# Two DRAM bounces of batch 2 issued ahead of the output weights, in a fused attention and snake-MLP kernel

## The chip, the cores and the metric

The kernel runs on one core of one Trainium2 chip. The metric is the device time in microseconds of one execution, the median over several runs. The profile is of one further execution, with its own time. In the code batches count from 0, so "the third batch" of the change is batch 2; the numbers below are those of the code.

## The reference

Attention with a relative-position bias over 8 batches, 8 heads, 576 positions and head size 64, and then a two-layer network with the snake activation on its 4608 x 512 result:

```python
scores = scale * np.matmul(q, k.transpose(0, 1, 3, 2))
scores = scores + bias.transpose(2, 0, 1)[None, :, :, :]
scores = scores - np.max(scores, axis=-1, keepdims=True)
attn = np.exp(scores)
attn = attn / (np.sum(attn, axis=-1, keepdims=True) + 1e-09)
x = np.matmul(attn, v)            # heads side by side: 4608 x 512
h = x @ w_in                      # 512 x 2048
s = np.sin(alpha * h)
g = h + s * s / (alpha + 1e-09)
return (g @ w_out).astype(np.float32)   # 2048 x 512
```

All inputs are float32; the kernel computes in float16 with float32 sums.

## The kernel before

**Stages.** The kernel goes through the batches t = 0 to 7. Attention of a batch runs over four pairs of heads p. For each pair TensorE (PE) forms the transposed scores (`sc`, from `kT` and `qT`, key chunks 0 to 3, a tail `t` from `kt`, and chunk 4 with the last 64 queries), ScalarE takes the exponential into `u` (L705), VectorE multiplies the part near the diagonal by the bias factor `m2r` or `mhr` (L730, L713), PE multiplies by `v` and `vh` into `am` (the attention-value products), and VectorE divides by the sums (L784, L785). The result goes transposed into `xT`: for batch 0 with PE and a copy, from batch 1 on with a transposing DMA on SP from `xp` (L815).

The network works on blocks b of 512 tokens. Input matmuls give 16 chunks of h (`sc<-xT,w_in`), ScalarE takes the sine (L865), ScalarE or VectorE the square (L872, L874), and VectorE adds it to h in `g` (L879), which also frees the PSUM bank of that chunk. Output matmuls (`am<-w_out,g`) sum over the 16 chunks f of `g` for each of four groups of 128 tokens, a copy to `outs` follows (L536, L538) and a DMA to `out` (L929). Block 0 is put in after the attention of batch 0; after batch 1 there is none, and block 1 follows the attention of batch 2. So the attention of batches 1 and 2 comes back to back, and the 64 output matmuls of block 0 are spread through it as filling work (L919, `fill`).

**Who sets the order.** The order of instructions on each engine is fixed when the kernel is built. `Plan` keeps tasks with estimated durations, dependences, priorities and a due time `nb` before which the plan does not start them, and emits them in the order in which its own clock would run them. On the chip only that order and the semaphores count; the due times act through the order alone. Some due times stand for the landing of a DMA that is issued outside the plan: `T_TR1` for the natural loads of k and q of batch 1, `T_V` for v of batches 0 and 1, `T_WO` for the four quarters of `w_out` (quarter f // 4 for output matmul f).

**The DMA queues.** Loads that change float32 to float16 go through POOL, whose DMA instructions share one software queue (q0). SP issues through a hardware queue (q1): transposing loads, copies of the tail of `kT` into `kt` (L385), and the results. The opening part of POOL is written out by hand, ahead of the plan. It ends with `load_w_in16`, two natural loads of k and q for batch 1 (`nat2`, L426), `load_v32(1)` (six loads to `v1st`, L408 and L411), `load_w_out16` (four quarters, L436) and `cast_v(1)` (six casts of `v1st` to `v` and `vh`, L416 and L419). `v1st` is needed because `w_out16` lends its space to v of batch 0 until that is cast.

From batch 2 on, k and q take another way. `stage_kq(t)` (L377) copies k and q of batch t from DRAM to DRAM, as float16 with the heads side by side (`staged_k`, `staged_q`): these are the bounces. `load_kqT(t)` then has SP load them transposed into `kT` (L389) and `qT` (L390) and fills `kt`. The buffers of `kT`, `qT`, `kt`, `v` and `vh` are double, by t % 2. For batch 2 the bounce is issued in `first` of batch 0, at the start of its scores in the plan, which on POOL's queue is behind `cast_v(1)`; `load_v16(2)`, `load_kqT(2)` and `stage_kq(3)` come in `first` of batch 1. From batch 3 on a task of the plan on SP, `ahead`, does this.

## Time and profile before

| | us |
|---|---|
| median of 8 runs | 394.9 |
| lowest and highest run | 391.36, 396.79 |
| the profiled execution, its own time | 392.74 |
| its span in the profile | 391.0 |

The span covers all but 1.7 us of the profiled execution's own time. All times inside the execution are microseconds from the start of the span. TensorE ran at full clock throughout.

| DMA (POOL) | issued at | time to landing |
|---|---|---|
| `nat2` k, q | 21.77, 22.55 | 14.5, 16.7 |
| last load to `v1st` | 33.72 | 10.7 |
| `w_out`, four quarters | 36.59, 39.58, 41.03, 41.97 | 10.1, 9.7, 11.1, 12.5 |
| `staged_k`, `staged_q`, batch 2 | 46.16, 47.89 | 12.1, 14.1 |
| `staged_k`, `staged_q`, batch 3 | 58.72, 62.41 | 19.0, 22.9 |

On SP, the transposing loads of batch 2 hold the queue from 58.30 (`kT`, 5.95) and from 64.31 (`qT`, 7.73).

How to read it: an issue is the time at which POOL writes the descriptors, the landing is when the semaphore tells that all data have arrived; with a queue that is full most of the time to landing is spent behind other DMAs. In a busy row "x" counts instructions. In a chain of work each line is start, length and what ran; a line that names a DMA is time in which the chain waited for that transfer. In a row of DMA packets the columns are packets, megabytes and the time that the packets took as a share of 16 engines; with several packets in flight on one engine that share goes over 100%.

### The profile page before, as it was taken

Reading aid. Unit: us, or ns where it says so; the run is one execution under the profiler, and the core shown is the slowest. Engines: PE = TensorE matmul, PEld = TensorE weight load, DVE = VectorE, ACT = ScalarE, POOL = GpSimd, SP = SyncE. Lnnn points to the kernel's source line nnn. Section 1 sums busy time; section 2 is a strip of 40 time slices with the busy share of each in tenths; the row PEclk is TensorE's granted clock in tenths of the full one; section 3 lists DMA queues with packets and bytes.
Section 4 is the critical chain, followed back from the end, with each engine's and each line's share of the span. In section 5 each row is a group of like instructions: output and inputs, shape, how many; then the busy total and the mean of one; then the engine's idle time right before and its main releaser. Section 6 shows DMA issues by size and latency. Waiting matters only on the chain.

```text
span 391.0 us, 8534 instructions
## 1 busy us (share of the span) xinstructions
PE 375.2 (96%) x3381; PEld 188.2 (48%) x3381; DVE 261.6 (67%) x584; ACT 322.5 (82%) x453; POOL 82.3 (21%) x96
## 2 busy tenths in 40 slices
PE   5989899999999999999999999999999999999995
PEld 2456445455544554455445544554455444444442
DVE  3676986767886679668966786679667949429100
ACT  2876999899999999999999999999999959539211
POOL 5672864063720044006300310000000000000000
PEclk9999999999999999999999999999999999999999
DMA  9999999999999969949992397210121000020112
GB/s 164 198 207 219 209 176 149 151 185 151 147 162 158 150 90 149 186 75 90 133 172 77 38 66 183 85 24 9 54 57 50 14 27 28 29 80 2 60 74 80
DMA packets 151207, 42.58 MB, mean 109 GB/s; under 512 B 140344, under 2 KB 145552, under 8 KB 151168
## 3 DMA queue, kind: packets, MB, share of 16 engines
q0 software_dynamic: 89872, 19.04, 58.9%
q1 hardware_dynamic: 61072, 22.95, 32.0%
q8 instruction: 26, 0.43, 0.5%
q14 instruction: 13, 0.11, 0.1%
q10 hardware_dynamic: 224, 0.05, 0.1%
HBM read 37.76 MB, written 16.52 MB: 139 GB/s over the span
## 4 chain that ended last, share of the span: by engine, by line
PE 82%; DMA 8%; ACT 4%; DVE 3%; issue 1%; POOL 1%; ACTq 0%; SPq 0%; DVEq 0%
PE sc L450 40%; PE am L450 34%; PE ca L450 4%; PE cb L450 4%; ACT u L705 3%; DMA qT<-staged_q 3%; DMA m2r<-e_dram 2%; DMA e_dram<-e_sb 1%; DMA phi_sb<-phi_const 1%; DVE g L879 1%; DVE outs L538 0%; DVE kT L538 0%; DVE xp L785 0%; POOL mhr L471 0%; DVE sq L874 0%
## 5 line engine op out<-in xcount | busy, mean ns | idle before, releaser
L705 ACT ACTIVATE u<-sc 128x1024 f16<-128x1024 f32 (+1 forms) x192 | 157.3, 897 | 14.1 <-PE sc L450 12.5
L450 PE MATMUL sc<-xT,w_in 128*128 128x512 f16 x576 | 132.6, 379 | 0.9 <-DVE g L879 0.6
L879 DVE SCALAR_TENSOR_TENSOR g<-sq,inv_a,sc 128x512 f16<-128x512 f16 x144 | 103.1, 745 | 24.0 <-PE am L450 16.6
L450 PE MATMUL am<-w_out,g 128*128 128x512 f16 x448 | 116.2, 380 | 0.3 <-DVE outs L538 0.2
L865 ACT ACTIVATE s<-sc,alphaT 128x512 f16<-128x512 f32 x144 | 93.0, 678 | 5.5 <-PE sc L450 4.2
L730 DVE TENSOR_TENSOR u<-u,m2r 128x512 f16<-128x512 f16 (+2 forms) x160 | 68.1, 440 | 31.5 <-ACT u L705 27.0
L450 PEld LDWEIGHTS <-w_in 128*128 128x128 f16 x576 | 55.2, 98 | 64.9 <-issue 1.8
L450 PEld LDWEIGHTS <-g 128*128 128x128 f16 x576 | 53.4, 98 | 66.2 <-issue 12.5
L450 PEld LDWEIGHTS <-u 128*128 128x128 f16 x1440 | 55.8, 98 | 17.2 <-issue 8.7
L450 PE MATMUL am<-v,u 128*128 128x65 f16 x1216 | 53.6, 194 | 0.0
L450 PE MATMUL sc<-qT,kT 64*128 64x64 f16 (+1 forms) x512 | 49.3, 295 | 2.8 <-ACT u L705 1.9
L872 ACT ACTIVATE sq<-s 128x512 f16<-128x512 f16 x79 | 49.2, 628 | 2.2 <-DVE g L879 0.5
L396 POOL DMA_DIRECT2D v<-in_v_dram x24 | 22.2, 1064 | 117.2 <-PE am L450 117.2
L450 PE MATMUL am<-vh,u 128*128 128x130 f16 x152 | 33.9, 223 | 1.0 <-DVE xp L785 0.8
L874 DVE TENSOR_TENSOR sq<-s 128x512 f16<-128x512 f16 x65 | 27.7, 428 | 5.2 <-ACT s L865 4.4
L450 PEld LDWEIGHTS <-kT 64*128 64x128 f16 x512 | 14.6, 95 | 29.9 <-issue 25.6
L785 DVE TENSOR_TENSOR xp<-am,rd 128x384 f16<-128x384 f32 (+1 forms) x56 | 27.5, 491 | 2.0
L784 DVE RECIPROCAL rd<-am 128x6 f32<-128x6 f32 (+1 forms) x60 | 11.2, 186 | 22.6 <-PE am L450 22.2
L538 DVE COPY outs<-am 128x512 f32<-128x512 f32 x21 | 14.4, 688 | 6.1 <-PE am L450 6.0
L937 ACT ACT_TABLE_LOAD x13 | 16.7, 1283 | 0.2
L377 POOL DMA_DIRECT2D staged_q<-in_q_dram x6 | 15.5, 2583 | 4.4 <-DMA staged_q<-in_q_dram 4.4
L536 ACT ACTIVATE outs<-am 128x512 f32<-128x512 f32 x7 | 4.2, 594 | 13.6 <-PE am L450 13.6
(87 smaller groups left out, 167.9 us busy)
## 6 DMA issues: line engine op xcount, KB each, us to landing
out_dram<-outs SPq DMA_DIRECT2D x36, 256.0 KB, 2.2
staged_k<-in_k_dram POOLq DMA_DIRECT2D x6, 576.0 KB, 16.5
staged_q<-in_q_dram POOLq DMA_DIRECT2D x6, 576.0 KB, 20.8
v<-in_v_dram POOLq DMA_DIRECT2D x24, 128.0 KB, 6.8
w_in<-in_moe_w_in_dram POOLq DMA_DIRECT2D x4, 512.0 KB, 9.7
w_out<-in_moe_w_out_dram POOLq DMA_DIRECT2D x4, 512.0 KB, 10.6
xT<-xp SPq DMA_TRANSPOSE x72, 3.5
w_out<-in_v_dram SPq DMA_DIRECT2D x4, 256.0 KB, 8.6
```

The costliest lines, as they stand in the source:

```text
L377: nc.gpsimd.dma_start(out=dst.ap()[t].rearrange("s (h d) -> s h d", h=H), in_=src[t].rearrange("h s d -> s h d"),)
L396: nc.gpsimd.dma_start(out=vs[t % 2][:, c, :, 0:D], in_=vp[128 * c : 128 * c + 128],)
L450: nc.tensor.matmul(out=out, lhsT=lhsT, rhs=rhs, start=start, stop=stop)
L538: k_of(e).tensor_copy(out=o, in_=i)
L705: nc.scalar.activation(out=o, in_=x, func=AF.Exp, scale=0.125)
L730: nc.vector.tensor_tensor(out=io, in0=io, in1=m2[:, 2 * p : 2 * p + 2, x0 : x0 + hi - lo], op=ALU.mult,)
L785: nc.vector.tensor_tensor(out=y.rearrange("p c (z d) -> p c z d", z=2), in0=a[:, :, :, 0:D], in1=r.unsqueeze(3).to_broadcast([128, nq, 2, ...
L865: nc.scalar.activation(out=s16.v, in_=h.v, func=AF.Sin, scale=alphaT[:, f : f + 1])
L872: nc.scalar.activation(out=sq.v, in_=s16.v, func=AF.Square)
L874: k_of(e).tensor_tensor(out=sq.v, in0=s16.v, in1=s16.v, op=ALU.mult)
L879: nc.vector.scalar_tensor_tensor(out=gcell[b].v[:, f, :], in0=sq.v, scalar=inv_a[:, f : f + 1], in1=h.v, op0=ALU.mult, op1=ALU.add,)
L937: nc.scalar.preload_act_table_set(name)
```

## The change

The bounces of batch 2 are issued by hand between `load_v32(1)` and `load_w_out16`, instead of in `first` of batch 0. `load_kqT(2)` leaves `first` of batch 1 and becomes a task of its own on SP, which the plan may place once the copies into `kt` for batch 1 are placed, with due time `T_KQ2`. The due times for v of batch 1, for the natural loads of batch 1 and for the quarters of `w_out` are set later. No operation is added or taken away.

```diff
-T_V = (18.5, 45.0)
-T_TR1 = (33.0, 37.0)
+T_V = (18.5, 50.0)
+T_TR1 = (36.0, 38.5)
+T_KQ2 = 50.0
...
-T_WO = (48.5, 50.5, 52.5, 54.0)
+T_WO = (56.0, 59.0, 62.0, 65.0)
...
     load_v32(1, P_)
+    stage_kq(2)
     load_w_out16()
     cast_v(1, P_, range(6))
...
         def first(t=t):
             if t == 1:
                 load_v16(t + 1)
-                load_kqT(t + 1)
-            if t < 2:
                 stage_kq(t + 2)
...
+        if t == 1:
+            aheads[2] = plan.add({"SP": 0.1}, lambda e: load_kqT(2), list(split_of.values()),
+                                 PB - 1000000, nb=T_KQ2)
```

## The prediction

> **What bounds the kernel now.** I read the busy times first, then the chain of work in order of time around the edit, then the waits and the busy time of short stretches there, and last the DMA views of the same stretch.

> ```profile
> PE 375.2 (96%) x3381; PEld 188.2 (48%) x3381; DVE 261.6 (67%) x584; ACT 322.5 (82%) x453; POOL 82.3 (21%) x96
> ```

> ```profile
> 54.42 0.26 PE cb L558 x12
> 54.68 2.48 PE am L450 x11
> 57.16 0.34 PE sc L450 x2
> ...
> 63.98 0.28 SPq L389
> 64.25 0.06 issue
> 64.31 13.34 DMA qT<-staged_q
> 77.65 0.14 issue
> 77.79 0.61 PE sc L450 x4
> ```

> The chain (start, length, what) goes through `qT<-staged_q`: the scores of batch 2 start when its queries have landed. That looks like 13 us to win, but the waits of 57.1 to 98 us tell what the landing really held up:

> ```profile
> ACT u L705 <- PE sc L450: 2.0, 4, 1.1
> PE sc L450 <- ACT u L705: 1.6, 6, 0.4
> PE sc L450 <- DMA qT<-staged_q: 0.7, 1, 0.7
> ...
> PE am L450 <- ACT u L705: 0.2, 1, 0.2
> ```

> TensorE lost 0.73 us to it (ScalarE 1.07 us, the longest of its four waits). Busy time by stretch (length, then PE, PEld, DVE, ACT, POOL):

> ```profile
> 57.10:97.00 39.90, 37.38 (x514) 20.85 (x514) 27.30 (x78) 37.67 (x48) 13.63 (x10) 1.00 1.96 159
> 99.00:116.00 17.00, 16.75 (x109) 7.93 (x105) 15.26 (x27) 16.52 (x27) 9.21 (x8) 1.00 1.98 155
> 177.00:217.00 40.00, 39.94 (x378) 20.29 (x377) 29.78 (x68) 37.64 (x53) 9.24 (x8) 1.00 1.23 110
> ```

> PE idles 2.5 us in the two attention stretches of batches 1 and 2, and next to nothing later: from 97 us to the end its listed waits sum to 1.4 us. So **PE's work is conserved**: a microsecond of PE work moved out of one place must find an idle microsecond before 97 us, or the end moves with it.

> [...]in the 0.73 us wait for qT, output matmuls whose data were there stood behind the scores and did not run. [...]here one output matmul reads 379 ns, but 16 in a row take 3.45 us in the chain, so I price it at 0.216 us. [...]From 72 to 76 us, with both queues full, the trace shows 1,694 packets of the gathering queue (q0) and 1,633 of the hardware queue (q1)[...].

> **The change part by part.**

> *1. Order on POOL and q0.* The two bounces (L377) go ahead of the four weight loads (L436) and six casts; no DMA is added. POOL's timeline before:

> ```profile
> 36.59 0.76 POOL L436 DMA_DIRECT2D w_out<-in_moe_w_out_dram  x1 [2.24 <-DMA nat<-in_k_dram]
> 39.58 0.75 POOL L436 DMA_DIRECT2D w_out<-in_moe_w_out_dram  x1 [2.24 <-DMA nat<-in_q_dram]
> ...
> 46.16 2.21 POOL L377 DMA_DIRECT2D staged_k<-in_k_dram  x1
> 47.89 2.71 POOL L377 DMA_DIRECT2D staged_q<-in_q_dram  x1
> ```

> The bounces inherit the waits for the natural loads of k and q and issue at 36.6 and 39.6, to 42.3; then four weight issues of 0.75 (to 45.3) and casts of 2.48 + 1.05, to 48.9 instead of 46.2. The casts feed the attention-value products of batch 1, first run at 62.0: 13 us of cover, cost nothing. The v loads of batch 2 follow on POOL at about 48.9. The bounces of batch 3 wait for the DMAs that used their semaphores last: w_out's last two quarters instead of the bounces of batch 2, so some 3 us later than 58.7 and 62.4. They landed at 77.7 and 85.3, and their transposing loads issue at 87.9 and 93.1: covered.

> q0 serves its DMAs in turn and is full. By time to landing, v1st ends at 44.4, w_out lands at 46.7, 49.3, 52.1 and 54.5, staged_k at 58.3, staged_q at 62.0. Rates:

> ```profile
> q0 software_dynamic: 1219, 1.21, 120.9%
> ```

> That is 44 to 50 us, nearly all w_out: 1,219 packets of 1 KB, so a quarter of 512 packets takes 2.5 us. From 52 to 62 us, mostly bounces, it is 11,790 packets in 10 us, so a bounce of 4,608 takes 3.9 us. After: staged_k lands at 48.2, staged_q at 52.

> *2. The transposing loads.* SP issues kT then qT after the kt loads at 47.3, so kT at 48.2 instead of 58.3. Before, hardware packets came some 4.6 us after that issue (none from 60 to 62); so from 52.8 they run beside w_out. Price of sharing: a w_out packet is 6 x 16 / 1219 = 79 ns of an engine, a bounce packet 13.6 ns, and 72 to 76 us leaves (64 - 1694 x 0.0136) / 1633 = 25 ns for a transposing one. One to one, a quarter takes 512 x 104 / 16 = 3.3 us: **w_out lands at about 54.9, 58.2, 61.5, 64.8**. If engine time rather than packets is shared, a quarter takes 5 us: 56, 61, 66, 68.5. The 2,304 packets of kT end by about 66 and those of qT, beside v, by about 74; PE asks for qT at about 77.5. The 0.73 us wait goes. The v loads land some 6 us later than 69.3, still ahead of the products that read them at about 84, and the bounces of batch 3 behind them by about 91, ahead of 93.1 by little, but the scores that need them start at 116. SP's xp transposes, held until 74.1 before, start sooner; their readers run after 97.

> *3. PE's order.* The due times of w_out (56 to 65) make the plan put the 11 output matmuls of 54.68 to 57.16 behind the first scores. The order of instructions after is: transposes, scores x4, output x4 (f 0 to 3), scores x4, tail x2, output x4, and so on; 35 output matmuls stand ahead of the scores of batch 2 instead of 43, and all 64 stand ahead of the same point as before, the eight input matmuls that start at 96.86. From there the order is the same. Do the scores fill the hole? No: the second pair needs the bank that this frees:

> ```profile
> 56.51 0.74 DVE L879 SCALAR_TENSOR_TENSOR g<-sq,inv_a,sc 128x512 f16<-128x512 f16 x1
> ```

> So PE can run two scores (0.27 us) and then idles to 57.25. ScalarE gains nothing either: its table load ends at 57.42 in both.

> *4. The sum, at 96.86 us.* Displaced: 11 x 0.216 = +2.39. First two scores early: -0.27. Wait for qT: -0.73. Of the other 1.8 us of PE waits, 0.96 falls in batch 1, where the new order leaves similar holes (few output matmuls early, since the scores still need the exponentials); 0.8 falls in batch 2, where the displaced matmuls now lie, and I take 0.6 of it as filled. **Sum +0.8 us**; with w_out in time it lies between 2.39 - 0.27 - 0.73 - 1.8 = -0.4 (every wait filled) and +1.4 (none). PE first needs w_out at 57.6 (f 0), 59.6 (f 4), 63.3 (f 8), 65.8 (f 12), from where the same neighbours ran before; margins 2.7, 1.4, 1.8, 1.0 us. After 97 nothing absorbs it. Against its own profiled time of 392.74 that is 393.5; the median of the runs shown is 2.2 us above it, and the same step puts it at 395.7.

> **The rivals.**

> *w_out late (slower).* Packets are not shared as in 72 to 76 us, or qT's follow kT's at once, and the second value of step 2 holds. PE then stands at f 4 for 1.4 us and at f 8 for 66 - 63.3 - 1.4 = 1.3 us, with scores queued behind, so ScalarE starves too. It decides once the second quarter lands after 59.6. For it: margins of 1 to 2.7 us in a stretch where landings take 10 to 23 us. Against: the equal packet counts. Time: 395.7 + 2.7 = 398.4.

> *The wait for qT is usually longer (faster).* Runs go from 391.4 to 396.8; DMA is full from 0 to 77 us and the landing sits on the chain. If the 2.2 us by which the median exceeds the profiled run are this wait, it is 2.9 us; with all 1.8 us of other waits filled the sum is 2.39 - 0.27 - 2.9 - 1.8 = -2.6, so 392.3. Against: nothing shows where the slower runs lose their time.

> *qT does not come sooner.* Hardware packets started only as staged_q ended; if q0 keeps them out until v is through, the wait stays: +1.5, 396.4. It counts with the forecast.

> **How the numbers follow.** 0.5% is 2 us, about what a measurement of this kernel can tell from no change. Forecast (+0.8) 0.47: within 0.37, slower 0.07, faster 0.03. w_out late 0.31: slower 0.29, within 0.02. Longer wait 0.22: faster 0.19, within 0.03. Together faster 0.22, within 0.42, slower 0.36. The likeliest is 395.7, its own range 394.5 to 396.4; the range over the cases is 392.3 to 398.8.

> **What would show it.** Right: no `qT<-staged_q` in the chain near 77 us; PE idle about 2 us between 54.7 and 57.3, put down to `g` (L879); fewer PE waits for `u` from 78 to 97; the eight input matmuls starting at about 97.7. Wrong: a PE wait for `w_out` at 58 to 67 us (first rival), or input matmuls starting before 96.5 (PE was not conserved). If the profiled span hardly moves and the median falls by 2 us, the second rival holds.

## The result and the profile after

| | before | after |
|---|---|---|
| median in the same series | 395.54 (53 runs) | 392.40 (18 runs) |
| lowest and highest | 391.36, 398.09 | 391.06, 393.75 |
| the profiled execution, its own time | 392.74 | 392.05 |
| its span | 391.0 | 390.3 |

The changed kernel is faster: the ratio of comparable runs is 0.9938, 95% interval 0.9913 to 0.9962. (The ratio leaves out executions far above the shortest of their kernel, so it is nearer to 1 than the two medians.) The forecast was 395.7, a loss of 0.8 on the 394.9 known then; 392.4 lies below its own range (394.5 to 396.4) and at the lower edge of the range over the cases (392.3 to 398.8). What moved is less the short executions, 391.4 against 391.1, than the long ones, 398.1 against 393.8. Of the 53 runs of before, 13 lie at 391.4 to 393.2 and 40 at 394.2 to 398.1, with none between. (In the 152 later runs of the same kernel the gap is thin, not empty: 9 lie in it.) The profile of before shown above belongs to the small group.

The page of the kernel after, its busy row and the row of the granted clock (tenths of full speed, 40 slices of 9.8 us):

```profile
PE 374.9 (96%) x3381; PEld 187.7 (48%) x3381; DVE 261.2 (67%) x584; ACT 322.8 (83%) x453; POOL 82.1 (21%) x96
PEclk8599989999999999999999999999999999999999
```

The same work as before. The 8 and 5 at the front are the opening, which ran at half clock from 7.8 to 21.4 us here and at full clock in the profile of before; the other 8 lies at 49 to 59 us, and to that I return. The chain of work around the edit (start, length, what):

```profile
54.80 0.67 DVE g L881
55.47 0.04 issue
55.51 0.60 PE sc L451 x2
56.12 1.82 PE am L451 x4
...
75.07 1.40 PE am L451 x6
76.47 0.54 PE sc L451 x4
77.00 1.44 PE am L451 x29
```

`qT<-staged_q` is gone from it: the scores of batch 2, at 76.4, follow output matmuls without a gap. What is late in its place is `g`, the last chunk of the network's first half, whose bank the second pair of scores needs. From the waits of 54 to 98 us (total, times, longest):

```profile
ACT u L707 <- PE sc L451: 2.5, 7, 0.9
...
PE sc L451 <- DVE g L881: 1.6, 1, 1.6
...
PE am L451 <- DVE xp L787: 0.4, 1, 0.4
...
PE am L451 <- ACT u L707: 0.2, 1, 0.2
```

No line for qT, one of 1.6 us for `g`, and the six waits of scores for `u` (1.6 us before) are gone: the displaced output matmuls fill them, helped here by a slower PE (clock 0.50 up to 59.0 us; in e10 below, the same order at full clock, two of them, 0.5 us, remain). The timeline of POOL of the kernel after (in brackets the idle time ahead and what ended it) shows when the new order was carried out:

```profile
35.43 2.21 POOL L378 DMA_DIRECT2D staged_k<-in_k_dram  x1 [2.10 <-DMA nat<-in_k_dram]
38.84 2.21 POOL L378 DMA_DIRECT2D staged_q<-in_q_dram  x1 [1.20 <-DMA nat<-in_q_dram]
40.55 3.48 POOL L437 DMA_DIRECT2D w_out<-in_moe_w_out_dram  x4
...
54.23 0.63 POOL L402 DMA_DIRECT2D vh<-in_v_dram  x1 [2.03 <-DMA w_out<-in_moe_w_out_dram]
57.62 0.61 POOL L402 DMA_DIRECT2D vh<-in_v_dram  x1 [2.76 <-DMA w_out<-in_moe_w_out_dram]
61.22 2.20 POOL L378 DMA_DIRECT2D staged_k<-in_k_dram  x1 [2.99 <-DMA w_out<-in_moe_w_out_dram]
64.29 2.20 POOL L378 DMA_DIRECT2D staged_q<-in_q_dram  x1 [0.87 <-DMA w_out<-in_moe_w_out_dram]
```

Each of the last four lines waited for one quarter of `w_out`, so they date the landings: 54.2, 57.6, 61.2, 64.3. The transposing loads on SP's queue, and the packets of 54 to 56 us:

```profile
46.61 10.04 SPq L390 DMA_TRANSPOSE kT<-staged_k  x1
...
56.70 8.94 SPq L391 DMA_TRANSPOSE qT<-staged_q  x1
```

```profile
q0 software_dynamic: 314, 0.31, 90.7%
q1 hardware_dynamic: 317, 0.08, 30.2%
```

By their times to landing (18.5 and 17.2 us) kT is there at 65.1 and qT at 73.9, 2.5 us ahead of need. 314 packets of one queue to 317 of the other: here too packets were shared one to one.

### The profile page after: what moved, and what is told of

It is laid out like the page before. It is cut to its first block, busy times and chain, and to the rows that moved or that the text cites. A ratio compares the mean times of both kernels' runs of the same rounds, so it can differ in the third digit from the quotient of the medians.

```text
span 390.3 us, 8536 instructions
## 1 busy us (share of the span) xinstructions
PE 374.9 (96%) x3381; PEld 187.7 (48%) x3381; DVE 261.2 (67%) x584; ACT 322.8 (83%) x453; POOL 82.1 (21%) x96
## 3 DMA queue, kind: packets, MB, share of 16 engines
HBM read 37.76 MB, written 16.52 MB: 139 GB/s over the span
## 4 chain that ended last, share of the span: by engine, by line
PE 91%; ACT 3%; DVE 3%; DMA 1%; issue 1%; ACTq 0%; DVEq 0%
PE sc L451 43%; PE am L451 38%; PE ca L451 4%; PE cb L451 4%; ACT u L707 2%; DMA phi_sb<-phi_const 1%; DVE g L881 1%; PE cb L560 1%; PE am L560 1%; ACT s L867 1%; DVE xp L787 0%; DVE kT L540 0%; DVE outs L540 0%; ACT sq L874 0%; DVE rd L786 0%
## 5 line engine op out<-in xcount | busy, mean ns | idle before, releaser
L881 DVE SCALAR_TENSOR_TENSOR g<-sq,inv_a,sc 128x512 f16<-128x512 f16 x144 | 103.2, 746 | 24.1 <-PE am L451 16.6
L451 PEld LDWEIGHTS <-w_in 128*128 128x128 f16 x576 | 55.1, 98 | 64.3 <-issue 1.0
L451 PE MATMUL sc<-qT,kT 64*128 64x64 f16 (+1 forms) x512 | 49.3, 297 | 3.0 <-DVE g L881 2.2
L397 POOL DMA_DIRECT2D v<-in_v_dram x24 | 21.2, 898 | 114.9 <-PE am L451 113.5
```

Source lines behind the costliest of these rows:

```text
L397: nc.gpsimd.dma_start(out=vs[t % 2][:, c, :, 0:D], in_=vp[128 * c : 128 * c + 128],)
L451: nc.tensor.matmul(out=out, lhsT=lhsT, rhs=rhs, start=start, stop=stop)
L881: nc.vector.scalar_tensor_tensor(out=gcell[b].v[:, f, :], in0=sq.v, scalar=inv_a[:, f : f + 1], in1=h.v, op0=ALU.mult, op1=ALU.add,)
```

## The experiments

**Theory A**: in most executions of the kernel before, PE waits about 3 us for qT, not 0.7, because the landing does not move with the compute; the change takes that wait away and pays with the displaced output matmuls and the hole (PE's idle time around the first two scores of batch 1). After the first runs the theory got its second half: after such a wait PE's clock is halved for some microseconds. **Rival B**: the gain comes from the new order of PE, or an accident of the runs; where a run tests something else, its expectation names B anew.

**1. The kernel before once more, and the parts of the change alone.**

e1 is the kernel before, unchanged.

> The kernel before, unchanged, for the profile of an execution nearer its median of 395.5 than the one shown (392.7). Theory A (in most executions the scores of batch 2 wait for qT much longer than the 0.73 us of the profile shown): an execution of 394 to 397 us shows TensorE waiting 2 to 5 us for the staged loads between 76 and 82 us, and a stretch of lower TensorE clock after it is possible. Rival B (the slow executions lose their time in the opening, where the bias factors arrive by DMA, or spread over the kernel): that wait stays at 1 us or less and the difference to the profile shown is already there at 57 us, or comes after 97 us. Time: about 395.5 for both.

395.14 (22 runs, 391.33 to 397.53), ratio 1.0022 (0.9994 to 1.005). Its profile fell on a short execution (span 390.5): wait for qT 0.90, landing 77.2.

e2 keeps the new order and puts the bounces back:

```diff
     load_v32(1, P_)
-    stage_kq(2)
     load_w_out16()
...
                 load_v16(t + 1)
+            if t < 2:
                 stage_kq(t + 2)
```

> All of the change but the place of the bounces: the due times, the task for the transposing loads and so the order on TensorE are those of the changed kernel, the bounces of batch 2 stay behind the output weights and the casts. Theory A (the gain is the wait for qT, which the new place of the bounces takes away; the new order on TensorE by itself costs the displaced output matmuls): the wait stays, the hole at 55 us is there too, 1.7 us of output matmuls are left for after the wait: about 397, slower than before by 1 to 2. Rival B (the new order on TensorE is what gains): about 392.4, as the changed kernel.

394.88, ratio 1.001 (0.9981 to 1.004): not the 397 of A nor the 392.4 of B. The order alone gains nothing, so the gain is the earlier qT. Nor does the order show its cost. One line of PE's timeline, the waits of 54 to 98 us and a stretch (length, then busy time of PE, PEld, DVE, ACT, POOL; behind them the granted clock):

```profile
55.86 0.39 PE L451 MATMUL sc<-qT,kT 64*128 64x512 f16 x2 [1.58 <-DVE g L880]
```

```profile
PE sc L451 <- DMA qT<-staged_q: 2.9, 1, 2.9
PE sc L451 <- DVE g L880: 2.2, 2, 1.6
```

```profile
56.00:58.00 2.00, 1.77 (x11) 0.53 (x10) 0.46 (x2) 2.00 (x3) 0.00 (x0) 1.00 2.46 157
```

The last `g` ends at 55.80 and the scores of batch 2 are due at 75.77, 19.97 us later, hardly more than before: eight output matmuls fewer stand ahead of them, and the hole stands there instead. Then they wait for the landing, as in the long executions of before. What was displaced comes behind it: the way from the scores to the input matmuls takes 21.26 us, 0.75 more than in e7 below (the kernel before with a similar wait), and that is less than the interval of the ratio can tell. The hole is as long as in the changed kernel, but here the clock stayed at 1.00 behind it.

e3 keeps the early bounces and gives the plan the due times of before:

```diff
-T_V = (18.5, 50.0)
-T_TR1 = (36.0, 38.5)
+T_V = (18.5, 45.0)
+T_TR1 = (33.0, 37.0)
...
-T_WO = (56.0, 59.0, 62.0, 65.0)
+T_WO = (48.5, 50.5, 52.5, 54.0)
```

> The bounces ahead of the output weights as in the changed kernel, but all due times as before, so TensorE runs 11 output matmuls ahead of the first scores of batch 1 while the weights land at about 54, 58, 61 and 64. Theory A (order on the queue and order on TensorE belong together): TensorE stands for the second and third quarter, the first scores start near 62 instead of 56, no wait for qT later; 4 us over the changed kernel, about 396.5. Rival B (the due times do not matter, the queue is all): within 1 us of the changed kernel, about 392.4.

399.61 (6 runs), ratio 1.0148 (1.0102 to 1.0194), against 396.5 expected. PE asks for `w_out` at 54 us and stands four times:

```profile
PE am L451 <- DMA w_out<-in_moe_w_out_dram: 5.9, 4, 2.3
```

and its clock reads 0.50 from 58 to 68 us. So with the early bounces the due times of before will not do.

e4 tries to spare the hole: two quarters of `w_out`, the bounces, the other two.

```diff
-T_WO = (56.0, 59.0, 62.0, 65.0)
+T_WO = (48.5, 50.5, 62.0, 65.0)
...
+    load_w_out16((0, 1))
     stage_kq(2)
-    load_w_out16()
+    load_w_out16((2, 3))
```

> Two quarters of the output weights, then the bounces of batch 2, then the other two quarters, with due times to match, so that eight output matmuls fill the hole ahead of the first scores of batch 1. Theory A (output matmuls displaced from the hole cost TensorE time that nothing gives back, and the hole lowers the TensorE clock): the hole is filled, qT lands some 5 us later than in the changed kernel but still ahead of its scores, 1 to 2 us under the changed kernel, about 390.8. Rival B (the hole is hidden behind ScalarE, which starts its exponentials no earlier): about 392.4. If qT becomes late again: 393 to 395.

393.36, ratio 0.9989 (0.9959 to 1.002): a miss. The hole moved, as the busy time by stretch shows:

```profile
56.00:58.00 2.00, 0.80 (x4) 0.38 (x4) 0.98 (x2) 2.00 (x3) 0.62 (x1) 1.00 1.22 198
58.00:60.00 2.00, 0.89 (x16) 0.48 (x16) 1.21 (x3) 2.00 (x4) 0.53 (x1) 1.00 1.24 192
60.00:62.00 2.00, 2.00 (x31) 1.35 (x27) 0.80 (x4) 1.18 (x3) 1.67 (x1) 0.53 1.62 134
```

The output matmuls that ran early are missing four microseconds later, where PE now waits for `u` (2.3 us in four waits, none longer than 0.6), and the clock falls to half at 60.1 us.

**2. Why most executions of before are longer.** e6 and e7 are two more profiles of the kernel before.

> The kernel before, unchanged, once more for the profile of an execution near its median. Theory A: if it takes 394 us or more, TensorE waits 2 to 5 us for qT near 77 us and its clock is lower for some microseconds after it; if it takes under 393, the wait is under 1.5 us. Rival B: a slow execution shows a wait for qT of 1 us or less.

> As the run before it: the kernel before, unchanged, for one more profile, with the same expectations of both theories.

395.45 and 395.36: both from the larger group. PE's timeline in e6, and its stretches:

```profile
77.78 1.04 PE L450 MATMUL sc<-qT,kT 64*128 64x512 f16 x4 [2.93 <-DMA qT<-staged_q]
```

```profile
76.00:78.00 2.00, 0.22 (x2) 0.16 (x4) 0.00 (x0) 0.00 (x0) 0.00 (x0) 0.76 1.86 209
78.00:80.00 2.00, 2.00 (x13) 0.69 (x10) 0.42 (x1) 1.57 (x2) 0.00 (x0) 0.50 1.72 165
80.00:82.00 2.00, 2.00 (x29) 1.41 (x26) 0.49 (x2) 0.37 (x1) 0.00 (x0) 0.50 1.88 240
82.00:84.00 2.00, 2.00 (x14) 0.94 (x13) 1.28 (x3) 1.99 (x3) 0.00 (x0) 0.54 1.53 107
```

The scores start at 77.78, within 0.01 us of the profile of before that was shown (77.79), but the wait ahead of them is 2.93 us and the four scores take 1.04 us instead of 0.61, at a clock of 0.50 that lasts to 84 us. All profiles side by side ("due" is the start of the scores of batch 2 less their wait for qT; in e9 it is where the zeros start):

| | last `g` ends | scores due | scores start | input matmuls start | scores to inputs | span |
|---|---|---|---|---|---|---|
| before, as shown | 57.25 | 77.06 | 77.79 | 96.86 | 19.07 | 391.0 |
| before, e1 | 56.63 | 76.44 | 77.34 | 96.41 | 19.07 | 390.5 |
| before, e6 | 55.05 | 74.85 | 77.78 | 99.60 | 21.82 | 393.7 |
| before, e7 | 55.97 | 75.78 | 78.97 | 99.48 | 20.51 | 393.6 |
| e9, zeros in the wait | 55.80 | 75.44 | 78.13 | 97.20 | 19.07 | 391.3 |
| e5, v held back | 55.15 | 74.89 | 74.89 | 93.96 | 19.07 | 388.1 |
| e12, the same | 57.33 | 77.06 | 77.06 | 96.13 | 19.07 | 390.2 |
| after | 55.46 | 76.40 | 76.40 | 96.15 | 19.75 | 390.3 |
| after, e11 | 55.30 | 76.25 | 76.25 | 95.99 | 19.74 | 390.1 |

Three things are read from it. From the last `g` to the scores being due takes 19.6 to 19.8 us in every row without the change. The span less the start of the input matmuls is 294.1 to 294.2 in all nine: nothing behind them gives or takes. And an opening that is earlier by 2.2 us (e6 against the profile shown) does not end earlier but 2.7 us later: the landing stays at 77.65, the wait grows from 0.73 to 2.93, and the half clock adds 2.75.

e8 makes the landing later, with one more bounce ahead of those of batch 2:

```diff
+            if t == 0:
+                nc.gpsimd.dma_start(
+                    out=spare.ap().rearrange("s (h d) -> s h d", h=H),
+                    in_=k[2].rearrange("h s d -> s h d"),
+                )
             if t < 2:
                 stage_kq(t + 2)
```

> The kernel before with one further DRAM bounce of 4,608 packets (k of batch 2 to a spare buffer) ahead of the two of batch 2, which delays qT by the 3.8 us that a bounce takes and nothing on TensorE. Theory A (the landing of qT ends last in most executions already): every execution now waits for it, the median goes to about 399 and the short executions of 391 to 393 are gone. Rival B (qT is at the edge only and most executions lose their time elsewhere): the wait adds to what is lost elsewhere only above 77 us, the median goes up by less than 3, to 396 to 397.

399.93 (4 runs), ratio 1.0136 (1.0075 to 1.0197), as A had it:

```profile
PE sc L451 <- DMA qT<-staged_q: 6.4, 1, 6.4
```

e9 keeps the wait and takes only the idle time out of it, with zeros that need no qT:

```diff
+                    if t == 2 and (p, i) == (0, 0):
+                        for _ in range(12):
+                            full(sc.v[:, 0, :], zz[:, 0:128], zz, True, True)
```

> The kernel before, with 12 matmuls of zeros (128x512, some 2.6 us at 0.216 each) put ahead of the scores of batch 2 into the PSUM bank that these scores then overwrite. They do not wait for qT, so they run where PE otherwise stands and waits for its landing at 77.2 to 78.8. Theory A (in most executions PE waits about 3 us for qT there, and the clock granted to it then halves for 4 to 6 us; executions with a wait of 0.7 to 0.9 us keep the clock and are the short ones): PE is busy through the wait, no slice at 78 to 84 us shows a clock near 0.50, the scores start with the landing or up to 2 us after it, and the time is 392.5 to 393.5 with a narrower spread than the kernel before. Rival B (only the length of the wait counts, the clock does not matter or halves anyway): 395 or, where the wait was short and the zeros push the scores back by 1.9 us, up to 397.

393.28 (22 runs, 392.50 to 395.51), ratio 0.9976 (0.9953 to 0.9998): 12 useless matmuls make the kernel before faster by 1.5 us in the median, though no score starts earlier for them. The transposing load, PE's timeline and the stretch after it:

```profile
63.17 7.49 SPq L390 DMA_TRANSPOSE qT<-staged_q  x1
```

```profile
75.44 2.75 PE L450 MATMUL sc<-zz 128*128 128x512 f16 x12
78.13 0.61 PE L450 MATMUL sc<-qT,kT 64*128 64x512 f16 x4
```

```profile
78.00:80.00 2.00, 2.00 (x34) 1.22 (x33) 0.38 (x1) 1.44 (x2) 0.00 (x0) 1.00 1.82 160
```

The clock stays at 1.00, and from the scores to the inputs it is 19.07 us again. But this profile alone does not show that the zeros did it: its qT had landed by 76.3 (13.1 us after the issue), so without them PE would have waited only about 1 us, and after 0.90 us in e1 the clock stayed up as well. What shows it is the mean granted clock, which was taken in every run. A stretch of 3.4 us at half clock takes 0.004 from that mean: e7, with 3.4 us of it, reads 0.995, and e6, with 6.8 us, 0.991. Runs by their mean clock (their median in brackets):

| mean clock | before, 152 runs | e9, 22 | after and e11, 40 | e10, 14 | e5 and e12, 20 |
|---|---|---|---|---|---|
| 0.998 to 1.000 | 25 (391.8) | 17 | 10 (391.7) | 12 | 17 |
| 0.994 to 0.996 | 59 (394.9) | 0 | 14 (392.6) | 0 | 0 |
| 0.986 to 0.991 | 37 (396.8) | 0 | 3 | 0 | 0 |
| 0.970 to 0.982 | 31 (394.8) | 5 | 13 | 2 | 3 |

The last row is what a half clock in the opening gives (the kernel after: 0.50 from 7.8 to 21.4 us and for 3.4 us behind the hole, mean 0.978); what came later in those runs can't be told from it. All 101 runs of before above 394.2 read 0.996 or less, and those that read 0.998 or more took 391.3 to 394.0. With zeros in the wait no run of 22 is left in the two middle rows; of the 34 runs of before beside them 23 are there. That shows the second half of the theory: PE's idle time, not the late qT as such, halved the clock, and the half clock (2.75 us in e6), not only the wait (2.93), made the long executions long. The same zeros make the shortest ones longer, 392.5 instead of 391.3.

**3. qT early without the change's price.** e5 is the kernel before, with the loads of v for batch 2, and behind them on POOL the bounces of batch 3, held back until qT has landed:

```diff
             if t == 1:
-                load_v16(t + 1)
                 load_kqT(t + 1)
+                nc.gpsimd.tensor_copy(out=hold, in_=qTs[0][:, 0, 0:4])
+                load_v16(t + 1)
```

> The kernel before with one small POOL copy that reads qT of batch 2, put ahead of the v loads of batch 2: POOL waits until qT has landed, so the transposing loads of batch 2 have the DMA engines for themselves. The order on TensorE, ScalarE, VectorE and SP is that of the kernel before, the output weights land as before. Theory A (the wait for qT is what the slow executions lose, and the change gained by taking it away, not by its new order on TensorE): qT lands near 73 instead of 77.6, the wait goes, no output matmul is displaced; 0.8 to 1.5 us under the changed kernel, about 391.2, and the spread of the times shrinks as it did there. Rival B (the slow executions of the kernel before lose their time elsewhere): about 394.5. Should v now be late for batch 2, there is a wait for v near 80 to 84 us.

390.55 (6 runs), ratio 0.9893 (0.9842 to 0.9943). POOL's timeline and the hardware queue from 62 to 64 us, in which q0 has no packet:

```profile
67.14 0.44 POOL L952 COPY hold<-qT 128x4 f16<-128x4 f16 x1 [17.52 <-DMA qT<-staged_q]
```

```profile
q1 hardware_dynamic: 1493, 0.37, 136.1%
```

1,493 packets in 2 us against 1,633 in 4 us (72 to 76) in the kernel before: alone on the DMA engines the transposing load ran nearly twice as fast, and qT is there by 67.1 instead of 76 to 79, from bounces that are no earlier (the load of kT, which follows them, starts at 57.8; at 56.9 to 58.3 before). The v loads are issued from 67.7 and the bounces of batch 3 at 72.4 and 74.1, and PE waits for none of them. From 72 to 76 us of before the v loads had landed (the last at about 70), so there it was a bounce of batch 3 that ran beside qT; what v and what the bounces cost was not tried apart. In the table e5's row has no wait and no displaced work.

e11 and e12 set the changed kernel and e5's kernel side by side.

> The changed kernel once more, unchanged, for a second profile and a direct comparison with the next one. Theory A: qT of batch 2 lands at 73 to 75 us, ahead of the scores at about 76.4; no wait of PE for it; the half clock at 56 to 59 us and a hole of about 1.6 us there again; 392.4 (ratio to the kernel before 0.993 to 0.995). Rival (its gain was an accident of one set of executions): ratio above 0.998.

> The kernel before with the v loads of batch 2 held back until qT has landed, once more, beside the changed kernel. Theory A: neither the wait for qT nor the displaced output matmuls and the hole of the changed kernel are in it, so it is below the changed kernel by 1 to 2 us: 390.5 to 391.3, no wait of PE over 0.5 us from 54 to 98 us, and qT at about 67 us. Rival: the 390.55 of six runs came from the few runs; it is then level with the changed kernel at 392.4.

e11: 392.45 (22 runs), ratio 0.9945 (0.9921 to 0.9969). e12: 391.07 (14 runs, 390.02 to 392.03), ratio 0.9914 (0.9881 to 0.9946). 18 of the 22 runs of the changed kernel lie above the longest of e12, though the two intervals against the kernel before overlap. Holding these loads back beats both kernels.

**4. The hole of the changed kernel.** PE's stretches in the kernel after:

```profile
54.00:56.00 2.00, 0.49 (x2) 0.09 (x1) 1.46 (x3) 1.97 (x3) 0.63 (x1) 0.89 1.21 195
56.00:58.00 2.00, 2.00 (x8) 0.56 (x8) 0.81 (x2) 1.59 (x2) 0.38 (x1) 0.50 1.22 197
```

Four output matmuls there take 1.82 us in the chain instead of 4 x 0.216. e10 puts 7 matmuls of zeros between the two pairs of scores:

```diff
+                    if t == 1 and (p, i) == (0, 0):
+                        x = new_ps("am1")
+                        for _ in range(7):
+                            full(x, zz[:, 0:128], zz, True, True)
```

> The changed kernel, with 7 matmuls of zeros (some 1.5 us at 0.216 each) between the first and the second pair of scores of batch 1, where PE idles 1.59 us until g (L881) frees the bank, and where the clock then reads 0.50 from 56 to 59 us. Theory A (the hole costs 1.6 us of idle time that the zeros can't give back, and about 1.2 us more through the halved clock): no 0.50 at 56 to 60 us, four output matmuls there take 0.86 us instead of 1.82, and the time is about 1.2 us below the changed kernel, 391.2. Rival B (the clock does not follow the idle time): the clock reads 0.50 as before and the time stays at 392.4, or rises a little where the zeros run past the point at which the bank is free.

392.14 (14 runs), ratio 0.9944 (0.9914 to 0.9975). The half of A on the clock holds. That it reads 1.00 in the profile says little, since e2 kept the clock without any zeros; but none of the 14 runs lies in the two middle rows of the table of clocks, where the changed kernel has 17 of 40. The 1.2 us do not come. PE's timeline says where they went in this execution:

```profile
54.04 1.68 PE L451 MATMUL am<-zz 128*128 128x512 f16 x7
...
64.83 1.02 PE L451 MATMUL am<-w_out,g 128*128 128x512 f16 x4 [0.78 <-DMA w_out<-in_moe_w_out_dram]
```

In the kernel after these four (f 12 to 15) run at 64.85 without a wait, 9.39 us after the last `g`; here they could have run 8.42 us after it and wait 0.78 for the last quarter of `w_out`. So of 0.97 us gained by the clock 0.78 went to the next in line, the last landing of `w_out`. That landing was late in this execution: the POOL instruction that waits for it started at 65.09, against 64.29 in the kernel after. How much the half clock costs the changed kernel over many executions is thus only bounded: its runs at 0.998 or more and those at 0.994 to 0.996 lie 0.9 us apart in the median, but e10, which is rid of it, only 0.3 below the changed kernel (392.14; 392.40 and 392.45).

## Why the prediction was wrong

- **Step 1, queue order: right.** The bounces issue at 35.4 and 38.8 (36.6 and 39.6 said), the casts end at 47.3 (48.9). The kT load issues at 46.6, on the landing of `staged_k` (48.2 said).
- **Step 2, shared packets: right.** 54.2, 57.6, 61.2, 64.3 for the quarters of `w_out` (54.9, 58.2, 61.5, 64.8 said); 65.1 and 73.9 for kT and qT (66 and 74). Neither engine-time sharing nor "qT does not come sooner" held.
- **Step 3, PE's order: right in its shape.** Two scores, then a hole until `g` frees the bank. The opening was 1.79 us earlier in the profile after (last `g` at 55.46 against 57.25), as in e6 and e7 without the change; so times are compared from there. What it missed is the half clock behind the hole, which comes in some executions (not in e2's).
- **Step 4, the sum: wrong in one term, and right for this profile by two others that cancel.** From the last `g` to the input matmuls the profile shown took 39.61 us, after 40.69: +1.08, where +0.8 was said, inside its bounds. Without the term for qT the sum was 2.39 - 0.27 - 0.6 = +1.5; against e5, which has no wait for qT (38.81), it measures 40.69 - 38.81 = +1.9. Two sizes in it were off, against each other. The new order costs +0.9, not +1.5: 19.97 - 19.74 ahead of the scores of batch 2 (e2 has the same order and hole at full clock) and 19.75 - 19.07 behind them. And the half clock, which the sum did not have, adds 20.94 - 19.97 = +1.0. The term that failed is **"wait for qT: -0.73"**. In e6 it is -2.93 for the wait and -(21.82 - 19.07) = -2.75 for the clock, together with +1.82 (what the table gives: 20.94 - 19.80 ahead of the scores, 19.75 - 19.07 behind them) -3.86, and 40.69 - 44.55 is -3.86 too. In e7 it is -3.19 - 1.44 + 1.81 = -2.82. The medians differ by -3.1. (The 379 ns and the 16 in 3.45 us from which a matmul was priced are input matmuls; output matmuls give the same 0.216, 14 in 3.02 us.)
- **The same step put to the median.** "The median of the runs shown is 2.2 us above it, and the same step puts it at 395.7" was the fault in one sentence: it took a wait read from one execution as that of all, though its own time, 392.74, lies with three of the eight runs (391.4 to 393.1) and not with the five at 394.5 to 396.8.
- **The second rival was the case.** It had the wait at 2.9 us, which e6 and e7 show (2.93, 3.19), and its test came out as written: the span hardly moved (391.0 to 390.3) and the median fell, by 3.1. That its 392.3 came out so near was luck: its sum filled all other waits and had no half clock in it. "Against: nothing shows where the slower runs lose their time" weighed an absence in one profile as evidence, and gave it 0.22.
- **The first rival, `w_out` late,** did not happen with the new due times; e3 is what it looks like (5.9 us of waits). It is nearer than thought, though: e10 meets it at f 12 with 0.78 us.

That the landing does not follow the opening is shown in four profiles of before (77.2 to 78.8) and in e9 (76.3, with an opening like e7's), not in each run; the mean clock says of the runs of the larger group that PE was at half clock somewhere, not where. What makes the opening itself vary by 2.2 us, and the landing by 2.5, with the same code, was not tried. A half clock in the opening does not explain the first: the five profiles that give these figures (before as shown, e1, e6, e7, e9) have none there, and their last `g` ends at 55.05 to 57.25.

## What to carry to other kernels

When one profile shows a short wait for a transfer, ask whether the landing moves with the compute or is set by full queues; if it is set by the queues, the wait is the difference of two times that each vary by themselves (here the scores were due at 74.85 to 77.06 us and the landing came at 77.2 to 78.8), and a run list that falls into two groups is the sign to profile again before pricing it. A wait of about 3 us on PE cost up to twice its length here, through the clock that followed (2.93 and 2.75 us in e6). And before moving a transfer ahead of others, try to clear its path: here, holding back loads that had slack brought qT some 10 us earlier and displaced nothing.

## What the runs showed of the hardware

A pause of a given length may or may not do it. The hole was 1.58 us long in e2 and the clock stayed at 1.00; it was 1.59 in the kernel after and in e11, and the clock fell to 0.50. With the waits of 0.73 and 0.90 us for qT (before as shown, e1) it stayed at 1.00; with those of 2.93 and 3.19 (e6, e7) it fell. What decides it for a hole of 1.6 us was not shown.
